# Expert 6's rest rows and ins moved ahead of expert 7's first layer, and with them the clearing, the read-back and the branch of expert 7, in a routed two-expert MoE behind chunked attention

## The chip, the cores and the metric

One core of a Trainium2 chip. The metric is device time in microseconds (us) of one launch of the whole program, the median of several runs. Beside it stands one profiled execution, whose trace is read below. Engines are called as the profile calls them: PE (matmul), PEld (its weight loads), DVE (vector), ACT (scalar), POOL (GpSimd, which here mainly issues DMAs), SP (which issues transposing DMAs). A q behind an engine's name (POOLq) is its sequencer, which handles branches, semaphore waits and the like.

## The reference, cut to what matters

Attention in chunks gives x of 3072 rows by 512. Then each row goes to the two experts (of 8) with the highest noisy logits:

```
top2 = np.argpartition(-noisy_logits, 2, axis=1)[:, :2]
top2_w = softmax of the two logits
for e in range(E):                  # E = 8, D = 512, F = 1024
    for k in range(2):
        mask = top2[:, k] == e
        h = np.maximum(x[mask] @ w1[e], 0.0)
        out[mask] += top2_w[mask, k, None] * (h @ w2[e])
```

## The kernel before

The first part of the program (attention, gating, sorting of the rows) is not touched. It ends with every row on one of 28 lists, one for each pair of experts. Of a list the first 96 rows (MT) are its **main** rows. What a list holds beyond that is a **rest** row, handled once for each of its two experts.

The pairs are numbered so that an expert e has three lists that it shares with the next three experts, its **outs** (`out_of(e)`), three that it shares with the three before it, its **ins** (`in_of(e)`), and one that it shares with expert e+4 or e-4, its **q** list. The work of an expert is

- `mm1_main(e, out_of(e), hO)` and `mm1_main(e, in_of(e), hI)`: first layer for three lists at once (288 columns, 32 matmuls). ACT and DVE in turn apply the relu and write hO or hI. Four PSUM buffers (`p_h`) stand between PE and them.
- `mm1_rest(e, r=False)` and `mm1_rest(e, q=False)`: first layer of the q list, whose 96 rows are spread, 32 each, behind the 96 rows of the three lists in hO; and of the rest rows, 96 of which go behind the lists in hI and 64 to a buffer hB. For the rest rows ACT alone applies the relu (`engs=(0,)`).
- `outs(e)` and `ins_(e)`: second layer, by `mm2_tiles`: for each of three lists a **tile** of 8 matmuls of 128 rows (96 of the list, 32 q or rest rows) by 512. DVE (L1105) adds the 96 rows to what the pair's other expert left, and ACT (L1090) copies the other 32 rows aside, into `yr`. Then PE may use the tile's PSUM buffer again. There are two of these (`p_y`). `ins_(e)` has a fourth, shorter tile, `rest_tile`, for the 64 rows of hB (16 matmuls, L1151), which takes a `p_y` buffer too.
- `scale_q(e)` (DVE, L1128) and `finish_q(e)` (DVE, L1135): weight of the q rows and sum of its two experts, into `yq`.

Results go to DRAM by `put` (L983) and `put_rest` (L1000), one indirect DMA each, issued on POOL; the puts of main rows are collected in a list `later`, which `flush()` issues. A rest row has another expert's share in DRAM already: `clear_prev(e)` (ACT, L1180) fills two tiles pA and pB with zeros, `get_prev(e)` (POOL, L1009) gathers into them what stands in DRAM, and DVE adds the new share: yB (L1157, 64 rows in halves, with pB) and yr (L1171, 96 rows, with pA). These gathers wait until the rest puts of the expert before have landed.

All engines run what they are given in a fixed order (`manual_schedule`): the order in which the code below issues it. Behind the last expert stands a second block: every engine loads a count `nov` into a register (L1523) and branches (L1525). With a count over zero, `overflow()` would run; with this data the branch goes past it. At the join, POOL waits for all its earlier DMAs and raises their semaphores by what `overflow()` would have raised them (`INC_SWDGE_SEM` in the trace). Then `flush()` issues on POOL what is left in `later`.

The loop over experts before, with n = e + 1: `mm1_main(e, in)`, `clear_prev(e)`, gather of the next expert's rest rows, `flush()`, `get_prev(e)`, `outs(e)`, `mm1_rest(e, q=False)`, `mm1_main(n, out)`, `mm1_rest(n, r=False)`, `finish_q(e)`, `flush()`, `ins_(e)`. For the last expert (e = 7): `mm1_rest(7, q=False)`, `mm1_main(7, in)` with `clear_prev(7)` in its middle, `flush()`, `get_prev(7)`, `ins_(7)`, `outs(7)`, `finish_q(7)`; its nine puts are all left for the last `flush()`.

Of the kernel before, what the change touches and what calls it, by code (L numbers as in the profile page):

```python
# [23 lines left out]
def kernel(  # L24
# [21 lines left out]
    N = B * S  # L46
# [53 lines left out]
    MT = 96  # L100
# [946 lines left out]
    def in_of(e):  # L1047
        return [3 * ((e - 1 - k) % E) + k for k in range(3)]
# [13 lines left out]
    def mm1_main(e, ps, h, **kw):  # L1062
        for k0, r in runs(ps):
            n = len(r)
            st = r[1] - r[0] if n > 1 else 1
            stop = r[-1] + (1 if st > 0 else -1)
            sl = slice(r[0], stop if stop >= 0 else None, st)
            mm1(e, n * MT, lambda kp: xs[:, sl, kp, :] if n > 1 else xs[:, r[0], kp, :],
                [(0, n * MT, lambda f0, fk: h[:, f0:f0 + fk, k0:k0 + n, 0:MT])], **kw)
# [16 lines left out]
    later = []  # L1086
# [24 lines left out]
    def flush():  # L1111
        for f in later:
            f()
        later.clear()
# [28 lines left out]
    def ins_(e):  # L1143
        wA, wB, dA, dB, hA, hB_ = rest_of[e]
        pA, pB = prev.pop(e) if e else (None, None)

        def rest_tile():
            p = psY.tile([128, Dm], F32, name="p_y")[:, 0:Dm // 2]
            for f in range(FB):
                for g in range(2):  # L1150
                    nc.tensor.matmul(out=p[g * RU:(g + 1) * RU], lhsT=hB[:, f, :], rhs=w2(e, f, g * Dm // 2, Dm // 2),  # L1151
                                     start=(f == 0), stop=(f == FB - 1), tile_position=(0, g * RU))
            yB = yrp.tile([128, Dm // 2], F32, name="yB", bufs=1)
            if e == 0:
                nc.vector.tensor_scalar(out=yB, in0=p, scalar1=wB, scalar2=None, op0=Alu.mult)
            else:
                nc.vector.scalar_tensor_tensor(out=yB, in0=p, scalar=wB, in1=pB, op0=Alu.mult, op1=Alu.add)  # L1157
            return yB

        unit = yrp.tile([128, Dm], F32, name="yr")  # L1160
        mm2_tiles(e, in_of(e), hI, unit)
        if e == E - 2:
            flush()
        yB = rest_tile()
        later_rest = [partial(put_rest, yB, dB, outB, 2 * N), partial(put_rest, unit[0:MT], dA, out, N)]
        if e < E - 1:
            later_rest.pop(0)()
        if e == 0:
            nc.vector.tensor_scalar(out=unit[0:MT], in0=unit[0:MT], scalar1=wA, scalar2=None, op0=Alu.mult)
        else:  # L1170
            nc.vector.scalar_tensor_tensor(out=unit[0:MT], in0=unit[0:MT], scalar=wA, in1=pA[0:MT], op0=Alu.mult, op1=Alu.add)  # L1171
        if e < E - 1:
            later_rest.pop(0)()
        later.extend(later_rest)

    def clear_prev(e):
        pA = yrp.tile([128, Dm], F32, name="pA", bufs=1)
        pB = yrp.tile([128, Dm // 2], F32, name="pB", bufs=1)
        for to in (pA, pB):
            nc.scalar.copy(to, zero.to_broadcast(list(to.shape)))  # L1180
        prev[e] = (pA, pB)

    def get_prev(e):
        pA, pB = prev[e]
        get_rest(pA[0:MT], rest_of[e][4], out, N)
        get_rest(pB, rest_of[e][5], outB, 2 * N)
# [9 lines left out]
    def turn_q(e):  # L1196
        g = QP + e % 4
        pin(nc.sync.dma_start_transpose(out=x3[e % 2][:, :, 0:MT], in_=xt[g][0:MT]))
# [229 lines left out]
    with tc.manual_schedule(engines={ET.PE, ET.Activation, ET.DVE, ET.SP, ET.Pool}):  # L1428
# [45 lines left out]
        ins_(0)  # L1474
        for e in range(1, E):
            n = e + 1
            if n == E:
                mm1_rest(e, q=False, engs=(0,))
            if n == E:
                mm1_main(e, in_of(e), hI, amid={2: lambda: clear_prev(e)})  # L1480
            else:
                mm1_main(e, in_of(e), hI)
                clear_prev(e)
            if e in (1, 3):
                dx = rest_decode(n, 4 if e == 1 else E)
                for _ in range(3):
                    next(dx)
            new = gathers(in_of(e + 2)) + gathers(out_of(e + 2)) if e + 2 < E else []
            if e + 2 < 4:
                gather_main(QP + e + 2)  # L1490
            if n < E:
                rest_rows(n)
            flush()
            get_prev(e)
            load_next()
            if n == E:
                ins_(e)
            scale_q(e)
            outs(e)
            if n < E:  # L1500
                turn_rest(n)
            turns(new)
            if e + 2 < E:
                turn_q(e + 2)
            if n < E:
                mm1_rest(e, q=False, engs=(0,))
                mm1_main(n, out_of(n), hO)
                mm1_rest(n, r=False)
            finish_q(e)
            if n < E:  # L1510
                flush()
            if e == 1:
                for k in range(4, E):
                    rest_facts(k)
            load_next()
            if n < E:
                ins_(e)
# [40 lines left out]
```

## Time and profile before

| | us |
|---|---|
| median of 3 runs | 334.56 (334.29 to 336.42) |
| the profiled execution | 333.11 |
| its span, first to last instruction | 331.5 |
| outside of the span | 1.6 |
| PE busy | 278.4 (84%) |
| DVE, ACT, POOL busy | 185.7, 153.5, 209.0 |
| mean granted PE clock | 0.926 |

Times in the rows are us from the span's start. The views read below are the chain of work that ended last (followed back from the last instruction), the timeline of one engine (start, length, line, operation, and in brackets how long the engine was idle before it and what the profile takes for the releaser), and the instructions of one source line with those of the sequencers. The first matmul of the experts' first layer (L1032) starts at 127.4 us; the rows below are of the last 52 us, experts 6 and 7.

### The profile page before, as it was taken

To read this page: it belongs to the slowest core of one execution; us is meant where nothing else is said; L and a number is where in the kernel's file an instruction comes from. 1 tells how busy PE (TensorE), PEld (TensorE's weight loads), DVE (VectorE), ACT (ScalarE), POOL (GpSimd) and SP (SyncE) were. 2 spreads that over 40 slices of the span, in tenths; PEclk is the share of its full clock that TensorE was granted. 3 is DMA by queue.
4 is the path that set the end of the run, shared out by engine and by line. 5 is a ranking of instruction groups with operands and counts; after the bars stand their busy time and mean duration, and the time that the engine had idled before them with its cause. 6 is when DMAs were issued, how large, how long until landed. Compare 5 with 4: busy or idle time off the path is not lost.

```text
span 331.5 us, 9214 instructions
## 1 busy us (share of the span) xinstructions
PE 278.4 (84%) x3746; PEld 206.3 (62%) x3762; DVE 185.7 (56%) x418; ACT 153.5 (46%) x316; POOL 209.0 (63%) x304
## 2 busy tenths in 40 slices
PE   0566979888799578999999999999999999999920
PEld 0455867777677368866766775585676666767400
DVE  4765755979798885644653443835345345443520
ACT  5666644766676202535453453453543534525210
POOL 4679595999482457767768675743754744735370
PEclk9969797999979755999999999999999999999975
DMA  7999959988926513435587895998979789522141
GB/s 126 212 211 192 216 109 219 219 138 119 225 51 117 132 30 80 97 79 111 86 182 123 87 182 120 191 217 143 224 151 215 171 158 186 130 83 74 58 145 37
DMA packets 43501, 46.79 MB, mean 141 GB/s; under 512 B 20465, under 2 KB 33845, under 8 KB 43452
## 3 DMA queue, kind: packets, MB, share of 16 engines
q0 software_dynamic: 23024, 38.27, 60.3%
q1 hardware_dynamic: 19884, 7.83, 11.7%
q8 instruction: 31, 0.51, 0.6%
q14 instruction: 18, 0.15, 0.1%
q10 hardware_dynamic: 544, 0.03, 0.1%
HBM read 59.11 MB, written 11.33 MB: 212 GB/s over the span
## 4 chain that ended last, share of the span: by engine, by line
PE 59%; DMA 6%; DVE 6%; issue 3%; ACT 2%; POOL 1%; POOLq 0%; SPq 0%; DVEq 0%; ACTq 0%
PE p_h L1032 28%; PE p_y L1096 21%; DMA w_all<-mvn 5%; PE p_y L1151 2%; PE p_v L490 1%; POOL out_dram L983 1%; PE ps_o L630 1%; ACT pT L616 1%; PE p_t L461 1%; DMA xt<-xd,main_src 1%; ACT w_all L465 1%; PE p_xt L1204 1%; PE p_p L610 0%; PE p_x L652 0%; PE p_rank L338 0%
## 5 line engine op out<-in xcount | busy, mean ns | idle before, releaser
L1032 PE MATMUL p_h<-w_all 128*128 128x288 bf16 (+3 forms) x1120 | 97.5, 248 | 0.7 <-ACT w_all L465 0.5
L1032 PEld LDWEIGHTS <-w_all 128*128 128x128 bf16 x1120 | 83.6, 99 | 14.0 <-issue 2.1
L1096 PE MATMUL p_y<-w_all 128*128 128x512 bf16 x368 | 83.6, 379 | 2.1 <-DVE yq L1090 0.8
L1020 ACT ACTIVATE w_all<-p_h 128x288 bf16<-128x288 f32 (+3 forms) x137 | 46.8, 375 | 45.4 <-PE p_h L1032 42.3
L1096 PEld LDWEIGHTS <-w_all 128*128 128x128 bf16 x384 | 37.1, 98 | 43.6 <-issue 2.1
L437 POOL COPY w_all<-w_all 128x512 bf16<-128x512 bf16 (+1 forms) x59 | 42.9, 795 | 12.2 <-PE p_t L461 7.4
L1018 DVE TENSOR_SCALAR w_all<-p_h 128x288 bf16<-128x288 f32 (+1 forms) x65 | 30.7, 476 | 34.2 <-PE p_h L1032 34.0
L983 POOL DMA_INDIRECT out_dram<-y,main_dst x24 | 22.8, 949 | 18.6 <-DMA w_all<-in_moe_w_dram 5.8
L1105 DVE SCALAR_TENSOR_TENSOR y<-p_y,main_w,y 96x512 f32<-96x512 f32 x24 | 17.9, 747 | 26.0 <-PE p_y L1096 26.0
L978 POOL DMA_INDIRECT xt<-xd,main_src x28 | 26.0, 928 | 10.0 <-issue 7.0
L1090 ACT COPY yr<-p_y 32x512 f32<-32x512 f32 x24 | 13.9, 579 | 36.4 <-DVE y L1105 34.6
L1101 ACT ACTIVATE y<-p_y,main_w 96x512 f32<-96x512 f32 x24 | 16.4, 683 | 21.5 <-PE p_y L1096 21.5
L461 PE MATMUL p_t<-identf,w_all 128*128 128x128 f32 x120 | 19.0, 297 | 1.8 <-ACT pT L616 0.8
L1000 POOL DMA_INDIRECT out_dram<-yB,rd x8 | 9.3, 1160 | 16.8 <-DVE yB L1157 15.6
L1090 DVE COPY yr<-p_y 32x512 f32<-32x512 f32 x12 | 8.3, 694 | 19.8 <-ACT y L1101 19.8
L1262 POOL DMA_INDIRECT fr<-tdr,adr x16 | 16.0, 1000 | 4.9 <-issue 4.6
L978 POOL DMA_INDIRECT xt<-xd,rs x16 | 14.8, 925 | 6.7 <-issue 3.4
L490 PE MATMUL p_v<-identf,w_all 128*128 128x128 f32 x96 | 16.4, 312 | 2.8 <-ACT w_all L465 1.8
L643 DVE TENSOR_TENSOR w_all<-ps_o,rs 128x512 bf16<-128x512 f32 x24 | 15.7, 683 | 5.0 <-PE ps_o L630 4.2
L461 PEld LDWEIGHTS p_t<-identf,w_all 128*128 128x128 f32 x120 | 14.3, 152 | 3.5 <-issue 1.6
L465 ACT COPY w_all<-p_v 128x512 f32<-128x512 f32 x21 | 12.0, 587 | 9.1 <-PE p_v L490 9.0
L1090 DVE COPY yq<-p_y 32x512 f32<-32x512 f32 x12 | 8.3, 694 | 12.9 <-ACT y L1101 12.8
(237 smaller groups left out, 419.6 us busy)
## 6 DMA issues: line engine op xcount, KB each, us to landing
w_all<-in_moe_w_dram POOLq DMA_DIRECT2D x12, 1024.0 KB
w_all<-in_moe_w_dram POOLq DMA_DIRECT2D x16, 256.0 KB
w_all<-in_k_dram POOLq DMA_DIRECT2D x4, 768.0 KB
w_all<-in_q_dram POOLq DMA_DIRECT2D x4, 768.0 KB
w_all<-in_v_dram POOLq DMA_DIRECT2D x4, 768.0 KB
xd<-w_all SPq DMA_DIRECT2D x24, 128.0 KB
w_all<-mvn SPq DMA_DIRECT2D x24, 32.0 KB
w_all<-xt SPq DMA_TRANSPOSE x39
```

Of the source, the lines that this page charges most:

```text
L437: i = eng.tensor_copy(to, x)
L461: nc.tensor.transpose(out=p_t[:, s, :], in_=m.bitcast(F32)[:, s * 128:(s + 1) * 128], identity=identf)
L490: nc.tensor.transpose(out=p_v[:, i, c, :], in_=vT[:, c, c0:c0 + 128], identity=identf)
L978: pin(nc.gpsimd.indirect_dma_start(out=t[0:n].bitcast(I32), out_offset=None, in_=src_, in_offset=bass.IndirectOffsetOnAxis(ap=ix, axis=0)))
L983: i = nc.gpsimd.indirect_dma_start(out=out if rows is None else rows, out_offset=bass.IndirectOffsetOnAxis(ap=ix, axis=0), in_=y, in_offse ...
L1018: nc.vector.tensor_scalar(out=out_, in0=in_, scalar1=0.0, scalar2=None, op0=Alu.max)
L1020: nc.scalar.activation(out=out_, in_=in_, func=Act.Relu)
L1032: nc.tensor.matmul(out=o if len(xk.shape) == 2 else o.rearrange("p (j t) -> p j t", j=xk.shape[1]), lhsT=w_all[:, e % WR, kp * F + f * 128 ...
L1090: (nc.scalar.copy if eng else nc.vector.tensor_copy)(to, p[MT:128, :])
L1096: nc.tensor.matmul(out=p, lhsT=h[:, f, k, :], rhs=w2(e, f), start=(f == 0), stop=(f == FB - 1))
L1101: nc.scalar.activation(out=y[0:MT], in_=p[0:MT], func=Act.Copy, scale=wt)
L1105: nc.vector.scalar_tensor_tensor(out=y[0:MT], in0=p[0:MT], scalar=wt, in1=y[0:MT], op0=Alu.mult, op1=Alu.add)
```

## The change

Only the last two experts are touched. For e = 6 the order becomes: `mm1_main(6, in)`, `clear_prev(6)`, `flush()`, `get_prev(6)`, **`mm1_rest(6, q=False)`**, `outs(6)`, **`finish_q(6)`, `flush()`, `ins_(6)`, `flush()`**, `mm1_main(7, out)` with **`clear_prev(7)` in its middle, `get_prev(7)`**, `mm1_rest(7, r=False)`. For e = 7: `mm1_rest(7, q=False)`, `mm1_main(7, in)`, `ins_(7)` with its **`rest_tile` ahead of the three tiles**, `outs(7)`, `finish_q(7)`. In `ins_(6)` the put of the third list is held back behind the two rest puts.

```diff
@@ ins_ @@
+        if e == E - 1:
+            yB = rest_tile()
+            later.append(partial(put_rest, yB, dB, outB, 2 * N))
         unit = yrp.tile([128, Dm], F32, name="yr")
         mm2_tiles(e, in_of(e), hI, unit)
         if e == E - 2:
+            after = later.pop()
             flush()
-        yB = rest_tile()
-        later_rest = [partial(put_rest, yB, dB, outB, 2 * N), partial(put_rest, unit[0:MT], dA, out, N)]
+            later.append(after)
         if e < E - 1:
-            later_rest.pop(0)()
+            yB = rest_tile()
+            put_rest(yB, dB, outB, 2 * N)
...
+        later.append(partial(put_rest, unit[0:MT], dA, out, N))
         if e < E - 1:
-            later_rest.pop(0)()
-        later.extend(later_rest)
+            later.pop()()
@@ the loop over experts @@
             n = e + 1
+            before_last = n == E - 1
             if n == E:
                 mm1_rest(e, q=False, engs=(0,))
-            if n == E:
-                mm1_main(e, in_of(e), hI, amid={2: lambda: clear_prev(e)})
-            else:
-                mm1_main(e, in_of(e), hI)
+            mm1_main(e, in_of(e), hI)
+            if n < E:
                 clear_prev(e)
...
             if n < E:
                 rest_rows(n)
-            flush()
-            get_prev(e)
+                flush()
+                get_prev(e)
             load_next()
             if n == E:
                 ins_(e)
+            elif before_last:
+                mm1_rest(e, q=False, engs=(0,))
             scale_q(e)
             outs(e)
...
+            if before_last:
+                finish_q(e)
+                flush()
+                load_next()
+                ins_(e)
+                flush()
+                mm1_main(n, out_of(n), hO, amid={1: lambda: clear_prev(n)})
+                get_prev(n)
+                mm1_rest(n, r=False)
+                continue
             if n < E:
                 mm1_rest(e, q=False, engs=(0,))
                 mm1_main(n, out_of(n), hO)
```

**POOL, from expert 6's puts to the branch.** Before; `y` are puts of lists, `yB` and `yr` the rest puts, `pA` and `pB` the gathers of `get_prev(7)`, `nxt` the count that the branch tests:

```order
L983 DMA out_0_dram<-yq_4116,main_dst_3203 3072x512 [waits DMASW6_49,DVE_49]
L983 DMA out_0_dram<-y_5072,main_dst_3203 3072x512 [waits DMASW7_49,DVE_49]
L983 DMA out_0_dram<-y_4777,main_dst_3203 3072x512 [waits DMASW0_49,DVE_49]
L983 DMA out_0_dram<-y_4483,main_dst_3203 3072x512 [waits DMASW1_49,DVE_49]
L1000 DMA out_0_dram<-yB_5604,rd4_4404 6144x256 [waits DMASW2_49,DVE_49]
L1000 DMA out_0_dram<-yr_5544,rd4_4404 3072x512 [waits DMASW3_49,DVE_49]
L1009 DMA pA_5674<-out_0_dram,ri4_4406 96x512 [waits DMASW3_49,DMASW4_49,DMASW2_49,Activation_49]
L1009 DMA pB_5675<-out_0_dram,ri4_4406 128x256 [waits DMASW5_49,Activation_49]
L1523 TENSOR_LOAD nxt_3020 [waits DVE_49]
L1525 COMPARE_AND_BRANCH
```

And in the changed kernel:

```order
L983 DMA out_0_dram<-yq_4116,main_dst_3203 3072x512 [waits DMASW6_49,DVE_49]
L983 DMA out_0_dram<-y_5072,main_dst_3203 3072x512 [waits DMASW7_49,DVE_49]
L983 DMA out_0_dram<-y_4777,main_dst_3203 3072x512 [waits DMASW0_49,DVE_49]
L1000 DMA out_0_dram<-yB_5517,rd4_4404 6144x256 [waits DMASW1_49,DVE_49]
L1000 DMA out_0_dram<-yr_5460,rd4_4404 3072x512 [waits DMASW2_49,DVE_49]
L983 DMA out_0_dram<-y_4483,main_dst_3203 3072x512 [waits DMASW3_49]
L1009 DMA pA_5540<-out_0_dram,ri4_4406 96x512 [waits DMASW2_49,DMASW4_49,DMASW1_49,Activation_49]
L1009 DMA pB_5541<-out_0_dram,ri4_4406 128x256 [waits DMASW5_49,Activation_49]
L1538 TENSOR_LOAD nxt_3020 [waits DVE_49]
L1540 COMPARE_AND_BRANCH
```

The number of rows is the same. One list's put has gone behind the two rest puts; that the whole piece stands earlier against the other engines is seen only on these.

**POOL, from the join to the end of the program.** Before, behind the branch that skips `overflow()`:

```order
L1525 ISA [waits Pool_49,Pool_sequencer_49,DMASW4_49,DMASW5_49,DMASW3_49,DMASW6_49,DMASW2_49,DMASW7_49,DMASW1_49,DMASW0_49]
L1525 UNCONDITIONAL_BRANCH
L983 DMA out_0_dram<-y_5379,main_dst_3203 3072x512 [waits DMASW6_49,DVE_49]
L983 DMA out_0_dram<-y_5084,main_dst_3203 3072x512 [waits DMASW7_49,DVE_49]
L983 DMA out_0_dram<-y_4789,main_dst_3203 3072x512 [waits DMASW0_49,DVE_49]
L1000 DMA out_0_dram<-yB_5766,rd4_4404 6144x256 [waits DMASW1_49,DVE_49]
L1000 DMA out_0_dram<-yr_5715,rd4_4404 3072x512 [waits DMASW2_49,DVE_49]
L983 DMA out_0_dram<-y_3579,main_dst_3203 3072x512 [waits DMASW3_49,DVE_49]
L983 DMA out_0_dram<-y_3975,main_dst_3203 3072x512 [waits DMASW4_49,DVE_49]
L983 DMA out_0_dram<-y_4320,main_dst_3203 3072x512 [waits DMASW5_49,DVE_49]
L983 DMA out_0_dram<-yq_4449,main_dst_3203 3072x512 [waits DMASW6_49,DVE_49]
```

In the changed kernel, the first rows of the same piece (the last four are the same):

```order
L1540 ISA [waits Pool_49,Pool_sequencer_49,DMASW4_49,DMASW5_49,DMASW3_49,DMASW6_49,DMASW2_49,DMASW7_49,DMASW1_49,DMASW0_49]
L1540 UNCONDITIONAL_BRANCH
L1000 DMA out_0_dram<-yB_5732,rd4_4404 6144x256 [waits DMASW6_49,DVE_49]
L983 DMA out_0_dram<-y_5423,main_dst_3203 3072x512 [waits DMASW7_49,DVE_49]
L983 DMA out_0_dram<-y_5084,main_dst_3203 3072x512 [waits DMASW0_49,DVE_49]
L983 DMA out_0_dram<-y_4789,main_dst_3203 3072x512 [waits DMASW1_49,DVE_49]
L1000 DMA out_0_dram<-yr_5734,rd4_4404 3072x512 [waits DMASW2_49,DVE_49]
```

Nine puts stand behind the join in both; yB has gone from fourth to first. The ISA row is `INC_SWDGE_SEM`.

**DVE, expert 7's second layer.** Before: the three ins, the rest rows yB and yr, the scaling of q, the three outs, the sum of q:

```order
L1105 SCALAR_TENSOR_TENSOR y_5379<-p_y_5716,main_w_3208,y_5379 96x512 [waits DMASW0_49,PE_49]
L1105 SCALAR_TENSOR_TENSOR y_5084<-p_y_5727,main_w_3208,y_5084 96x512 [waits PE_49]
L1105 SCALAR_TENSOR_TENSOR y_4789<-p_y_5738,main_w_3208,y_4789 96x512 [waits PE_49]
L1157 SCALAR_TENSOR_TENSOR yB_5766<-p_y_5749,rg4_4405,pB_5675 128x256 [waits DMASW2_49,DMASW5_49,DVE_49,PE_49]
L1171 SCALAR_TENSOR_TENSOR yr_5715<-yr_5715,rg4_4405,pA_5674 96x512 [waits DMASW4_49,Activation_49]
L1128 TENSOR_SCALAR yq_4449<-yq_4449,main_w_3208 96x512
L1105 SCALAR_TENSOR_TENSOR y_3579<-p_y_5771,main_w_3208,y_3579 96x512 [waits PE_49]
```

In the changed kernel:

```order
L1157 SCALAR_TENSOR_TENSOR yB_5732<-p_y_5715,rg4_4405,pB_5541 128x256 [waits DMASW1_49,DMASW5_49,DVE_49,PE_49]
L1105 SCALAR_TENSOR_TENSOR y_5423<-p_y_5735,main_w_3208,y_5423 96x512 [waits DMASW0_49,PE_49]
L1105 SCALAR_TENSOR_TENSOR y_5084<-p_y_5746,main_w_3208,y_5084 96x512 [waits PE_49]
L1105 SCALAR_TENSOR_TENSOR y_4789<-p_y_5757,main_w_3208,y_4789 96x512 [waits PE_49]
L1175 SCALAR_TENSOR_TENSOR yr_5734<-yr_5734,rg4_4405,pA_5540 96x512 [waits DMASW4_49,Activation_49]
L1128 TENSOR_SCALAR yq_4449<-yq_4449,main_w_3208 96x512
L1105 SCALAR_TENSOR_TENSOR y_3579<-p_y_5771,main_w_3208,y_3579 96x512 [waits PE_49]
```

yB, which waits for the landing of pB (DMASW5), has gone from behind the three ins to ahead of them; yr and the scaling of q now follow the third in directly. On SP the order is the same.

## Prediction

> **What bounds the kernel now.** I read the chain that ended last first, from expert 6 on (start, length, what):
>
> ```profile
> 279.85 0.22 PE p_y L1096
> 280.12 4.91 PE p_y L1096 x22
> 285.03 7.49 PE p_h L1032 x96
> 292.58 5.13 PE p_y L1096 x23
> 297.71 0.99 PE p_y L1151 x16
> 298.70 6.24 PE p_h L1032 x64
> 304.94 0.22 PE p_y L1096
> 305.21 4.93 PE p_y L1096 x22
> 310.16 0.76 DVE y L1105
> 310.94 0.59 ACT yr L1090
> 311.56 0.75 DVE yr L1171
> 312.33 0.43 POOL out_dram L983
> ...
> 322.62 0.92 POOL out_dram L983
> ```
>
> Up to 310 us the chain is PE, piece after piece without a hole. Then it leaves PE, and from 312.33 on it is POOL alone. PE works until 316.91 (below), so the end isn't set by the matmuls but by POOL's puts. Their timeline:
>
> ```profile
> 301.30 0.93 POOL L1000 DMA_INDIRECT out_dram<-yr,rd  x1 [0.30 <-issue]
> 304.99 1.00 POOL L1009 DMA_INDIRECT pA<-out_dram,ri  x1 [2.76 <-ACT w_all L1020]
> 306.29 1.03 POOL L1009 DMA_INDIRECT pB<-out_dram,ri  x1 [0.30 <-issue]
> 312.33 1.19 POOL L983 DMA_INDIRECT out_dram<-y,main_dst  x1 [5.01 <-DVE yr L1171]
> ...
> 322.62 0.92 POOL L983 DMA_INDIRECT out_dram<-yq,main_dst  x1 [0.30 <-issue]
> ```
>
> POOL idles 5.01 us and then issues nine puts, the last eight 1.29 us apart on average ((322.62 - 312.33) / 8), the last with only 0.30 behind the one before: it is late with all of them. The profile names DVE's yr as what ended the idle time. But the first put's data is an in of expert 7, whose tile ended at 306.67 (304.94 to 305.21 + 4.93 for three tiles: 1.73 a tile), while yr is the fifth put. So I asked for the branch's line and the end's, sequencers included (count, lengths min/median/max, first and last start):
>
> ```profile
> L1525 POOLq EVENT_SEMAPHORE  x6: 17/30/43, 309.1 to 309.6; - x6
> ...
> L1525 POOLq COMPARE_BRANCH  x1: 58/58/58, 306.0 to 306.0; - x1
> L1525 POOLq INC_SWDGE_SEM  x1: 1735/1735/1735, 309.7 to 309.7; - x1
> ...
> L1525 ACTq COMPARE_BRANCH  x1: 50/50/50, 318.3 to 318.3; - x1
> ...
> L1525 ACTq EVENT_SEMAPHORE  x1: 17/17/17, 320.8 to 320.8; - x1
> L1553 POOLq DRAIN  x3: 46/109/11514, 319.1 to 331.2; - x3
> ```
>
> There it is: POOL branches at 306.0, next does something at 309.1, raises semaphores from 309.7 to 311.4, and starts the first put 0.9 later. That the releaser ended at 312.30 is chance. From branch to first put is **6.3 us**. ACT shows the same hole behind its branch (318.3 to 320.8) with nothing to wait for, so about 3 of the 6.3 us are the branch's own and not the landing of pB.
>
> **The change part by part.** No instruction is added or removed; pieces swap places.
>
> *PE.* The pieces from 279.85 on, by these rows: tiles of outs 5.18, ins 5.13, rest tile 0.99. First layer: the rest rows and ins of 7 take 6.24; the rest rows of 6 with the outs and q rows of 7 take 7.49. Three lists in 32 matmuls take 4.03 (the ins of 6, the row of the same chain just ahead of those above):
>
> ```profile
> 275.83 4.03 PE p_h L1032 x32
> ```
>
> That leaves 2.21 for rest rows and 1.25 for q rows. New order: rest 6 to 282.06, outs 6 to 287.24, ins 6 to 292.37, rest tile 6 to 293.36, first layer of 7 (4.03 + 1.25 + 2.21 + 4.03) to 304.88. Before it is 304.94: **0**, if nothing new stalls. Two places are tight. ACT gets expert 6's eight rest relus right behind the last in's relu and the clears, before the first out's `y`; four PSUM buffers take the four rest tiles, so PE doesn't wait, and ACT is done (about 283.4) when the first out's tile is (283.8). `finish_q(6)` now stands on DVE between outs and ins of 6 and holds the first in's sum by some 0.4 us, so its PSUM buffer comes free at about 290.7, just when the third tile wants it. And expert 7's clears now wait for yr of 6 (294.55), and ACT's next relu for the clears (1.0 us): its `p_h` buffer is free at 295.8, wanted at 295.9. I take 0.05 for these, bounds 0 and 0.5 (one PSUM stall as it stands in the row of 311.57 below, 0.46). Covers gone: beyond these margins each 0.1 us costs 0.1.
>
> *POOL up to the branch.* The puts of 6 stand behind the gathers and puts that fill POOL until 290.5:
>
> ```profile
> 279.44:290.51 11.07, 11.02 (x87) 7.50 (x86) 4.37 (x8) 5.79 (x17) 8.63 (x9) 1.00 0.53 135
> ```
>
> (9 of POOL's DMAs in 11.07 us, so 1.23 each.) The yq put goes at 290.8, two y at 292.0 and 293.3, yB at 294.5 (its data is done at 293.9), yr at 295.8, the third y at 297.0. pA waits for yr's landing: before, 304.99 - 301.30 = 3.69 after yr's start, so 299.5; pB at 300.8. The branch's hole and join then let the first put go 6.3 us after a branch at 300.5: **306.85**, bounds 303.9 (no hole of 3 us) and 309.5 (the hole twice). [...]
>
> *Expert 7's second layer.* Rows before:
>
> ```profile
> 311.16 0.48 DVE L1157 SCALAR_TENSOR_TENSOR yB<-p_y,rg,pB 128x256 f32<-128x256 f32 x1 [0.25 <-PE p_y L1151]
> 311.56 0.74 DVE L1171 SCALAR_TENSOR_TENSOR yr<-yr,rg,pA 96x512 f32<-96x512 f32 x1
> 312.22 0.48 DVE L1128 TENSOR_SCALAR yq<-yq,main_w 96x512 f32<-96x512 f32 x1
> 313.49 0.75 DVE L1105 SCALAR_TENSOR_TENSOR y<-p_y,main_w,y 96x512 f32<-96x512 f32 x1 [0.80 <-PE p_y L1096]
> ...
> 318.34 0.75 DVE L1135 SCALAR_TENSOR_TENSOR yq<-yr,main_w,yq 96x512 f32<-96x512 f32 x1 [0.65 <-ACT yr L1090]
> 311.57 5.34 PE L1096 MATMUL p_y<-w_all 128*128 128x512 bf16 x23 [0.46 <-ACT yr L1090]
> ```
>
> Before, PE stood 0.46 us ahead of the outs: the short rest tile ran out before ACT had emptied the third in's PSUM buffer. Now the rest tile goes first (304.94 to 305.94) and the ins end at 307.67, 309.40 and 311.13, with no stall. But what's late next comes at once. The third in's `y` and copy (0.75 + 0.58) end at 312.5, yr at 313.3, the scaling at 313.7, and only then does DVE take the first out, done by PE at 312.86. Its `y` and ACT copy end at 314.98, and the third out's tile, which wants that buffer, waits for them from 314.6. It starts at 315.03 and ends 1.88 later (like 311.57 to the first out's end, 313.45): **316.91, where it ended before** (311.57 + 5.34). The 0.46 is lost again. So yq is done at 319.09 as before (318.34 + 0.75); if expert 6 loses 0.05, at 319.14.
>
> *The last puts.* A put that finds POOL free starts 0.28 after its data (yq of expert 6: 292.36 + 0.74 to 293.38):
>
> ```profile
> 292.36 0.74 DVE L1135 SCALAR_TENSOR_TENSOR yq<-yr,main_w,yq 96x512 f32<-96x512 f32 x1
> 293.38 0.92 POOL L983 DMA_INDIRECT out_dram<-yq,main_dst  x1 [2.87 <-DVE yq L1135]
> ```
>
> With a first put at 306.85, POOL follows the tiles: yB 306.85, ins at 308.7, 310.5, 312.2, yr 313.6, outs at 314.9, 316.1, 318.0, and the last at 319.42 against 322.62: **3.20 us earlier**. POOL by itself would need the first put by 309.5 for that (319.42 less eight steps of 1.23), so it has 2.7 us in hand. The first put of before took 1.19 instead of 0.92 beside L1128; yr's put will run beside it, so I allow it 0.3, which the gaps behind it take up. [...]
>
> *Behind the last put.* From its end (323.54) to the span's end are 7.96 us, most of it POOL's DRAIN (319.1 to 330.6). I carry these, and the 1.6 outside of the span, along unchanged. The profiled execution would go from 333.11 to 329.9. The median of the runs shown is 1.45 above it; the difference is applied to it: 334.56 - 3.20 = **331.4**.
>
> **The rivals.**
>
> 1. *POOL stays behind.* The hole behind the branch, or the wait for the landings of yB and yr ahead of pA, takes over 2.7 us more than here, and the puts queue again. For it: POOL's piece up to the branch is full from 279.4 on. Against: POOL has to be late for eight puts. Up to half of the gain goes: 332 to 333.5.
> 2. *The end doesn't follow the last put.* DRAIN starts at 319.1, just when yq is done and long before the last put's start, and takes 11.51. If that length is its own, not a wait for the puts, the end stays with yq: 334.6. Against: four puts were still due at 319.1, and a drain that waits for them explains a start ahead of them.
> 3. *Slower: pB lands late.* DVE's yB waits for pB and now stands ahead of all six tiles. DVE takes its work in order, so a late pB holds the `y` of the ins, their PSUM buffers and PE. By the sum pB is issued at 300.8 and landed by 304.1 (before: started 306.29, its semaphore passed by 309.6), and is wanted at 306.0. PE first feels it when the second in's tile wants the rest tile's buffer, at 307.7. Slower than before begins where pB lands 3.2 us after that slack, at some 310.4, over 6 us late. If the gather waited for the landing of every put before it in a crowded queue, say until 314, the time would be 338.
> 4. *More than forecast.* If the third out's stall stays away, or part of the 7.96 shrinks once the puts no longer queue, 0.5 to 1.5 more: 330 to 330.9.
>
> That the change doesn't do what it says is unlikely: in the order, the branch stands right behind pB, and pB right behind expert 6's puts.
>
> **How the numbers follow.** Forecast 0.62, alone 330.9 to 331.9 (the tight PE places on one side, half a stall less on the other); rivals 0.12, 0.12, 0.06 and 0.08. The range from 329.9 to 334.5 takes in the first and the fourth rival and part of the second, leaving out about 0.16. One per cent, about what a measurement of this kernel can tell from no change, is 3.35 us, so 331.2: the forecast lies just inside. Of it 0.28 is below 331.2; with the fourth rival 0.36 faster. The rest of it and the first two rivals make 0.58 the same; the third, 0.06 slower.
>
> **What would show it.** In the profile after: the idle time of 5.01 ahead of the first put behind the join gone, POOLq's branch at 300 to 301, its join's INC_SWDGE_SEM ended by 306; yB's put first, at about 306.9; the last put at 319 to 320, waiting for yq and not for POOL; PE's first layer of 7 ended at 304.9 to 305.1; PE idle about 0.45 ahead of the third out and not of the first; 8 us from the last put's end to the span's. Wrong I am if INC_SWDGE_SEM ends after 309, if the 8 us change by over 0.5, or if DVE's yB waits for a DMA.

## The result, and the profile after

The changed kernel takes **332.14 us** (median of 20 runs, 329.45 to 335.07), the kernel before 334.55 in the same session (20 runs, 331.65 to 339.91). The ratio is 0.9932, 95% interval 0.9904 to 0.9960: some 2.3 us less, 1.3 to 3.2 by the interval. Forecast were 331.4 and 3.2 less. Ratios, here and below, leave out slowed runs, over 1.5% above the fastest of their kernel, so they can differ a little from the ratio of two medians.

| profiled execution, us | before | forecast | after |
|---|---|---|---|
| time / span | 333.11 / 331.5 | 329.9 / - | 330.17 / 328.5 |
| POOL's branch | 306.0 | 300.5 | 300.5 |
| first put behind it | 312.33 | 306.85 | 307.08 |
| PE's first layer of 7 ends | 304.94 | 304.93 | 305.03 |
| last put starts | 322.62 | 319.42 | 319.59 |
| its end to the span's end | 7.96 | 7.96 | 7.96 |

POOL's timeline of the changed kernel, from the last puts of expert 6 on (start, length, what, in brackets the idle time ahead of it):

```profile
295.88 0.93 POOL L1000 DMA_INDIRECT out_dram<-yr,rd  x1 [0.30 <-DVE w_all L1018]
297.11 0.92 POOL L983 DMA_INDIRECT out_dram<-y,main_dst  x1 [0.30 <-issue]
299.55 1.00 POOL L1009 DMA_INDIRECT pA<-out_dram,ri  x1 [1.51 <-ACT w_all L1020]
300.85 1.03 POOL L1009 DMA_INDIRECT pB<-out_dram,ri  x1 [0.30 <-ACT w_all L1020]
307.08 1.02 POOL L1000 DMA_INDIRECT out_dram<-yB,rd  x1 [5.20 <-DVE yB L1157]
308.92 0.95 POOL L983 DMA_INDIRECT out_dram<-y,main_dst  x1 [0.81 <-DVE y L1105]
310.64 0.92 POOL L983 DMA_INDIRECT out_dram<-y,main_dst  x1 [0.77 <-DVE y L1105]
312.37 0.92 POOL L983 DMA_INDIRECT out_dram<-y,main_dst  x1 [0.81 <-DVE y L1105]
313.76 0.92 POOL L1000 DMA_INDIRECT out_dram<-yr,rd  x1 [0.47 <-DVE yr L1175]
314.98 0.92 POOL L983 DMA_INDIRECT out_dram<-y,main_dst  x1 [0.30 <-issue]
316.21 0.92 POOL L983 DMA_INDIRECT out_dram<-y,main_dst  x1 [0.30 <-issue]
318.20 0.92 POOL L983 DMA_INDIRECT out_dram<-y,main_dst  x1 [1.07 <-DVE y L1105]
319.59 0.92 POOL L983 DMA_INDIRECT out_dram<-yq,main_dst  x1 [0.48 <-DVE yq L1135]
```

The idle time of about 5 us is still there, but it now lies ahead of the work. Before, 0.30 stood between all the puts (a queue). Now 0.5 to 1.1 do, with a DVE row named: POOL waits for tiles. Only the two puts behind yr's still stand 0.30 apart, and the queue is empty again before the third out's. The branch and the end, in the view of one line with its sequencers:

```profile
L1540 POOLq COMPARE_BRANCH  x1: 58/58/58, 300.5 to 300.5; - x1
L1540 POOLq INC_SWDGE_SEM  x1: 1735/1735/1735, 304.4 to 304.4; - x1
...
L1568 POOLq DRAIN  x3: 46/109/8257, 319.4 to 328.2; - x3
```

The end of the chain that ended last:

```profile
285.39 0.76 DVE y L1105
...
293.07 12.97 DMA out_dram<-y,main_dst
306.28 0.58 issue
307.08 1.02 POOL out_dram L1000
...
318.20 0.92 POOL out_dram L983
319.11 0.24 issue
319.36 1.15 POOLq L1568
```

It now leaves PE at 285.39 and runs through the join. The 12.97 us are no landing: that put's data had landed by 295.81, and 293.07 + 12.97 is 306.04, when the join's INC_SWDGE_SEM raises the same semaphore. So this chain is not what bounds: the first put could have gone earlier without moving the last one, as the kernel without the branch shows below.

The hole is as long as it was, 6.5 us from branch to first put (307.08 - 300.54) against 6.3. PE and DVE in expert 7's second layer:

```profile
304.96 1.06 PE L1151 MATMUL p_y<-w_all 128*64 128x256 bf16 x16
305.95 8.81 PE L1096 MATMUL p_y<-w_all 128*128 128x512 bf16 x40
315.25 1.89 PE L1096 MATMUL p_y<-w_all 128*128 128x512 bf16 x8 [0.49 <-ACT yr L1090]
...
306.06 0.48 DVE L1157 SCALAR_TENSOR_TENSOR yB<-p_y,rg,pB 128x256 f32<-128x256 f32 x1 [1.03 <-DMA out_dram<-yB,rd]
...
312.74 0.75 DVE L1175 SCALAR_TENSOR_TENSOR yr<-yr,rg,pA 96x512 f32<-96x512 f32 x1 [0.65 <-ACT yr L1090]
313.40 0.48 DVE L1128 TENSOR_SCALAR yq<-yq,main_w 96x512 f32<-96x512 f32 x1
...
318.56 0.75 DVE L1135 SCALAR_TENSOR_TENSOR yq<-yr,main_w,yq 96x512 f32<-96x512 f32 x1 [0.65 <-ACT yr L1090]
```

PE's stall has moved from ahead of the first out to ahead of the third, 0.49 long, and yq is done at 319.31. The mean granted clock is 0.943 against 0.926 before, but rows of the same work are equally long in the experts' part of both: 1.06 for a rest tile, 6.31 for 64 matmuls of the first layer. So the clock is not what shortened the last stage.

### The profile page after: what moved, and what is told of

It is laid out like the page before. It is cut to its first block, busy times and chain, and to the rows that moved or that the text cites. A ratio compares the mean times of both kernels' runs of the same rounds, so it can differ in the third digit from the quotient of the medians.

```text
span 328.5 us, 9225 instructions
## 1 busy us (share of the span) xinstructions
PE 279.1 (85%) x3762; PEld 205.7 (63%) x3762; DVE 185.5 (56%) x418; ACT 153.4 (47%) x316; POOL 210.3 (64%) x304
## 4 chain that ended last, share of the span: by engine, by line
PE 49%; DMA 9%; DVE 8%; POOL 6%; issue 4%; ACT 2%; POOLq 1%; DVEq 0%; ACTq 0%
PE p_h L1032 24%; PE p_y L1096 18%; DMA out_dram<-y,main_dst 4%; POOL out_dram L983 3%; DMA w_all<-mvn 2%; DMA xd<-w_all 2%; PE p_y L1151 2%; PE p_t L461 1%; POOL w_all L378 1%; POOL red L364 1%; DMA xt<-xd,main_src 1%; PE p_list L384 1%; DVE w_all L532 1%; ACT pb L603 1%; ACT pT L616 1%
## 5 line engine op out<-in xcount | busy, mean ns | idle before, releaser
L1032 PE MATMUL p_h<-w_all 128*128 128x288 bf16 (+3 forms) x1120 | 96.4, 247 | 0.9 <-DVE w_all L1018 0.5
L1032 PEld LDWEIGHTS <-w_all 128*128 128x128 bf16 x1120 | 82.8, 99 | 14.0 <-issue 2.5
L1096 PE MATMUL p_y<-w_all 128*128 128x512 bf16 x384 | 85.9, 379 | 1.2 <-DVE yq L1090 0.6
L1105 DVE SCALAR_TENSOR_TENSOR y<-p_y,main_w,y 96x512 f32<-96x512 f32 x24 | 17.9, 746 | 23.5 <-PE p_y L1096 23.5
L1101 ACT ACTIVATE y<-p_y,main_w 96x512 f32<-96x512 f32 x24 | 16.4, 683 | 22.0 <-PE p_y L1096 19.9
L461 PE MATMUL p_t<-identf,w_all 128*128 128x128 f32 x120 | 18.2, 287 | 1.6 <-ACT pT L616 0.8
```

Source lines behind the costliest of these rows:

```text
L461: nc.tensor.transpose(out=p_t[:, s, :], in_=m.bitcast(F32)[:, s * 128:(s + 1) * 128], identity=identf)
L1032: nc.tensor.matmul(out=o if len(xk.shape) == 2 else o.rearrange("p (j t) -> p j t", j=xk.shape[1]), lhsT=w_all[:, e % WR, kp * F + f * 128 ...
L1096: nc.tensor.matmul(out=p, lhsT=h[:, f, k, :], rhs=w2(e, f), start=(f == 0), stop=(f == FB - 1))
L1101: nc.scalar.activation(out=y[0:MT], in_=p[0:MT], func=Act.Copy, scale=wt)
L1105: nc.vector.scalar_tensor_tensor(out=y[0:MT], in0=p[0:MT], scalar=wt, in1=y[0:MT], op0=Alu.mult, op1=Alu.add)
```

## The experiments

My theory: the gain is POOL's time behind the branch, taken out of the way of expert 7's puts by the earlier clearing, read-back and branch; the rest tile's new place brings nothing by itself. The rival: it is the new order of tiles (PE's stall), and the branch is beside the point.

Single executions differ by several us in parts that no edit touches (in the profiled ones expert 0's first matmul starts anywhere from 127.4 to 134.1 us), so I compare the last stage. **L** is the start of the last put, **S** the end of the span, both counted from the end of the last L1032 matmul, which is where expert 7's first layer ends. The first four variants below (from "before, no branch" to "sums of yr and q moved") ran on a chip on which the kernel before takes 334.8 us; the others on two chips on which it takes 417 and 422. There PE waits for "issue" in the first layer's line, as in this row from the list of waits of the first kernel with early scaling (total us, times, longest),

```profile
PE p_h L1032 <- issue: 22.2, 19, 3.7
```

while all the idle time ahead of that group is 0.9 us in the changed kernel's profile above. That hides a gain of two us in the total, but not in the last stage.

| kernel | L | S | ratio to before, 95% |
|---|---|---|---|
| before | 17.68 | 26.56 | |
| after | 14.56 | 23.44 | 0.9932 [0.9904, 0.9960] |
| before, no branch | 14.42 | 23.22 | 0.9821 [0.9762, 0.9880] |
| after, no branch | 14.56 | 23.37 | 0.9931 [0.9880, 0.9981] |
| after, late clearing and branch | 15.93 | 24.81 | 0.9944 [0.9891, 0.9996] |
| after, sums of yr and q moved | 14.73 | 23.61 | 0.9891 [0.9831, 0.9951] |
| after, rest tile behind the ins | 14.43 | 23.30 | 0.9998 [0.9937, 1.0059] |
| before, rest tile first (two runs) | 16.41, 16.38 | 25.29, 25.25 | 1.0128 [0.9916, 1.0339], 0.9942 [0.9840, 1.0043] |
| after, rest rows of 6 behind the outs | 14.56 | 23.44 | 0.9987 [0.9940, 1.0033] |
| after, last puts by SP | - | 19.27 | 0.9962 [0.9879, 1.0045] |
| after, scaling of q early (three runs) | 14.17 | 23.05 | 1.0032 [0.9958, 1.0105], 0.9891 [0.9819, 0.9964], 0.9931 [0.9888, 0.9975] |

### Without the branch

```diff
-        with tc.issue_after(last[0].ins):
-            nov = nc.values_load(nxt[0:1, 0:1], ...
-        with tc.If(nov > 0):
-            overflow()
```

In the kernel before:

> The kernel before without the count's load, the branch and the overflow path behind it (left out: the rows beyond the rest rows' room, of which this data has none). Theory (the gain of the change is POOL freed from the branch's hole before expert 7's puts are due): the first put behind pB starts at about 307.7 instead of 312.33, the puts then follow the tiles, the last starts at 319.4 instead of 322.6, span 328.3, ratio to before 0.990: the whole gain without any reordering. Rival (the gain is in the new order of PE's work): no change, 331.5.

and in the changed one:

> The changed kernel without the branch (same part left out). Theory: in the changed kernel the hole behind the branch is hidden (POOL is ready at about 307.0, when yB is), so the last put stays at 319.6 and the span at 328.5, within 0.2. Rival (the branch still costs something there, at the end of the program too): 0.5 or more shorter.

POOL's timeline of the kernel before without its branch:

```profile
309.73 1.03 POOL L1009 DMA_INDIRECT pB<-out_dram,ri  x1 [0.30 <-issue]
311.18 0.95 POOL L983 DMA_INDIRECT out_dram<-y,main_dst  x1 [0.42 <-DVE y L1105]
...
315.85 1.18 POOL L1000 DMA_INDIRECT out_dram<-yB,rd  x1 [0.31 <-DVE yr L1171]
...
322.81 0.91 POOL L983 DMA_INDIRECT out_dram<-yq,main_dst  x1 [0.48 <-DVE yq L1135]
```

The order is the old one, late gathers included, yet the first put goes 0.42 behind pB and the last waits for yq. L is 14.42: taking the branch away gives the whole gain of the change in the last stage (3.26 against 3.12) without moving a tile. In the changed kernel the same edit gives nothing (14.56 both). So the two are one gain, and the rival falls. What the edit takes out is the whole block: the count's load, the branch, and the join with its waits and INC_SWDGE_SEM. The runs don't part these. The new order itself costs a little: from the start of expert 5's rest tile to the last put are 44.60 us in the old order without the branch, 45.00 in the new one with it or without. The total of the first, 329.75 us (6 runs), is 5.1 below the kernel before, 1.8 more than its last stage explains (by the ratio of the table it would be 6.0 below); its profiled execution (333.48) doesn't contain it, and it stays open.

### Late clearing and branch in the changed order

```diff
-            mm1_main(e, in_of(e), hI)
+            mm1_main(e, in_of(e), hI, **(dict(amid={2: lambda: clear_prev(e)}) if n == E else {}))
+            if n == E:
+                get_prev(e)
...
-                mm1_main(n, out_of(n), hO, amid={1: lambda: clear_prev(n)})
-                get_prev(n)
+                mm1_main(n, out_of(n), hO)
```

> The changed kernel with expert 7's clearing (and with it the read-back) back in the middle of the first layer of its ins, the rest tile still ahead of the ins. Theory: pA starts at 303.3 (the clearing's end) instead of 299.55, pB at 304.6, the branch at 304.3, the first put at about 310.6; pB lands at about 307.7, so DVE's yB ends at 308.3 instead of 306.5 and PE stalls some 0.7 ahead of the second in; the nine puts need the first by 309.5, so the last starts at 320.4: 0.8 to 1.0 later than in the changed kernel, 2.0 to 2.3 earlier than before. Rival (where the clearing stands does not matter): as the changed kernel, 328.5.

```profile
308.16 1.03 POOL L1009 DMA_INDIRECT pB<-out_dram,ri  x1 [0.30 <-ACT w_all L1020]
314.22 1.02 POOL L1000 DMA_INDIRECT out_dram<-yB,rd  x1 [5.02 <-DVE y L1105]
315.55 0.96 POOL L983 DMA_INDIRECT out_dram<-y,main_dst  x1 [0.31 <-issue]
316.81 1.25 POOL L983 DMA_INDIRECT out_dram<-y,main_dst  x1 [0.30 <-issue]
...
324.50 0.92 POOL L983 DMA_INDIRECT out_dram<-yq,main_dst  x1 [0.30 <-issue]
```

The branch comes at 307.84, 0.7 us ahead of the layer's end, instead of 4.5 ahead of it, and the queue of 0.30 gaps is back. 1.37 of the 3.12 are lost again, more than I had expected, since one put is also stretched. The third rival shows itself in small: DVE's yB waits for pB, and PE's next row of 40 matmuls takes 9.04 instead of 8.81, so it lost 0.23 where 0.7 had been expected.

```profile
310.93 0.48 DVE L1157 SCALAR_TENSOR_TENSOR yB<-p_y,rg,pB 128x256 f32<-128x256 f32 x1 [2.36 <-DMA pB<-out_dram,ri]
```

### The place of the rest tile

In the changed kernel put back behind the ins:

```diff
-        if e == E - 1:
-            yB = rest_tile()
-            later.append(partial(put_rest, yB, dB, outB, 2 * N))
         unit = yrp.tile([128, Dm], F32, name="yr")
...
+        else:
+            yB = rest_tile()
+            later.append(partial(put_rest, yB, dB, outB, 2 * N))
```

> The changed kernel with expert 7's rest tile put back behind its ins. Counted from the end of the first layer of expert 7's ins (305.0 in the changed kernel): theory (that the rest tile goes first gains nothing by itself): PE stalls 0.46 ahead of the first out as before, and not ahead of the third; the last put starts 14.4 after, as in the kernel before without its branch, against 14.56 in the changed one; the span ends at 23.3 against 23.44. Rival (putting the rest tile first is part of the gain): last put 15.0 or later.

In the kernel before put ahead of them (the opposite edit), run twice:

> The kernel before with nothing changed but expert 7's rest tile ahead of its ins. Theory: the branch stands where it did, so the first put starts 7.4 after the end of expert 7's first layer, the nine puts queue and the last starts at 17.7, as before (17.68): no gain. DVE's yB now waits for pB's landing until about 4.4, so PE stalls some 2.2 ahead of the second in, which the puts' queue hides; yq is done at 16.3 to 16.5. Rival (the gain is in the new order of the second layer): last put at 15 or earlier; rival (the late pB costs): later than 18.2.

> The kernel before with the rest tile of expert 7 first, once more. On the slow chip the branch stood 0.23 ahead of the end of the first layer, since PE itself was held there, and the last put came 16.64 after the branch, the same as before (322.62 - 305.98 = 16.64). Theory: where PE isn't held the branch is 1.0 after the first layer's end as before, the last put 17.7 after it, the span ends 26.6 after it: no gain, ratio 0.995 to 1.005. Rival (the rest tile's place gains by itself): 16.4 or less.

With the rest tile last the stall ahead of the first out is back, as expected (0.45), and L is 14.43, 0.13 less than in the changed kernel. With it first in the kernel before, L reads 16.4 both times, the figure that had been put down for the rival. But the condition of that figure, a PE that isn't held, was met in neither run: PE stood for 0.16 and 0.78 (0.18 and 0.79 in the first run) waiting for ACT within the first layer just ahead, and so the branch came 0.2 ahead of the layer's end instead of 1.0 behind it. From branch to last put the two runs take 16.64 and 16.60 (before: 322.62 - 305.98 = 16.64), and POOL's puts stand 0.30 apart to the end. PE pays for yB waiting for pB, as the second of these runs shows:

```profile
391.32 1.90 PE L1096 MATMUL p_y<-w_all 128*128 128x512 bf16 x8
393.75 7.07 PE L1096 MATMUL p_y<-w_all 128*128 128x512 bf16 x32 [0.53 <-DVE yB L1157]
```

So the tile's place gains nothing. In the changed order it costs a tenth: on one chip L is 14.56 with it first (the variant below) and 14.43 with it last.

### Rest rows of expert 6 behind its outs

```diff
-            elif before_last:
-                mm1_rest(e, q=False, engs=(0,))
             scale_q(e)
             outs(e)
...
             if before_last:
+                mm1_rest(e, q=False, engs=(0,))
                 finish_q(e)
```

> The changed kernel with expert 6's rest rows' first layer put back behind its outs (but still ahead of its ins). Theory (their place ahead of the outs is neither needed nor harmful: PE does the same work, and the ins find the relus done): from the end of the first layer of expert 6's ins to that of expert 7's ins 25.1 to 25.3 as in the changed kernel, last put 14.56 after that. Rival (the ins of 6 wait for ACT's relus of the rest rows when these come right ahead of them): 0.3 to 0.6 longer.

The last stage is that of the changed kernel (14.56 and 23.44), as it should be. From the end of the first layer of expert 6's ins to that of expert 7's are 35.1, neither the 25.1 to 25.3 of the theory nor the rival's 0.3 to 0.6 more. In expert 6's ins PE waited twice for ACT:

```profile
371.20 1.03 PE L1096 MATMUL p_y<-w_all 128*128 128x512 bf16 x2 [2.68 <-ACT w_all L1020]
375.42 7.71 PE L1096 MATMUL p_y<-w_all 128*128 128x512 bf16 x22 [3.19 <-ACT w_all L1020]
```

But ACT itself stood idle there for 2.94 and 3.73 us with nothing of this core named, on one of the slower chips. Whether the order or the chip made these waits isn't settled, nor what the rest rows' place ahead of the outs is worth.

### What bounds the last stage now

First, the sum of yr behind the first out's, and the scaling of q ahead of the rest tile:

```diff
-                ins_(e)
...
+                scale_q(e)
+                outs(e, amid={0: ins_(e)})
```

(`ins_` hands back yr's sum as a function, called behind the first out.)

> The changed kernel with two of DVE's sums of expert 7 moved out of the way of its first out: the scaling of q ahead of the rest tile's sum, the rest rows' sum yr behind the first out's y. Theory: DVE takes the first out as soon as PE ends it (313.1 instead of 313.8), so the stall of 0.49 ahead of the third out goes, PE ends at 316.6 instead of 317.1, yq is done at 318.8 and the last put starts at 319.1: 0.5 earlier than in the changed kernel, span 328.0, ratio to before 0.989. Rival (the last put is held by POOL, which then has yr's put behind the first out's): no change to the changed kernel.

PE's 48 matmuls run through in one row of 10.53 and yq is done 0.64 sooner, but the last put 0.17 later: yr's put now stands behind an out's, and two puts are stretched.

```profile
317.53 1.18 POOL L983 DMA_INDIRECT out_dram<-y,main_dst  x1 [0.81 <-DVE y L1105]
...
321.46 1.43 POOL L983 DMA_INDIRECT out_dram<-y,main_dst  x1 [0.30 <-issue]
323.19 0.92 POOL L983 DMA_INDIRECT out_dram<-yq,main_dst  x1 [0.30 <-issue]
```

POOL is the bound again by a hair, as the rival had it. So only the scaling is moved, yr stays:

```diff
             if n == E:
+                scale_q(e)
                 ins_(e)
-            elif before_last:
-                mm1_rest(e, q=False, engs=(0,))
-            scale_q(e)
-            outs(e)
+                outs(e)
+            else:
+                if before_last:
+                    mm1_rest(e, q=False, engs=(0,))
+                scale_q(e)
+                outs(e)
```

> The changed kernel with one of DVE's operations moved: the scaling of q of expert 7 ahead of the rest tile's sum. Theory: DVE takes the first out 0.4 sooner, PE's stall of 0.49 ahead of the third out shrinks to 0.1 or less, yr's put stays ahead of the outs' and starts beside no operation of DVE that reads only SBUF, so no put is stretched (in the run with both sums moved two were, by 0.26 and 0.51, and POOL took back the 0.6 that PE gained). Last put 14.0 after the end of expert 7's first layer instead of 14.56, span end 22.85 instead of 23.44. Rival (POOL's five last puts are the bound whatever DVE does): 14.5.

> The kernel with the scaling of q moved ahead of the rest tile's sum, once more: the run before found its chip a quarter slower in the whole expert part (before: 417 us), so that its total says little. Its last part measured 14.17 from the end of expert 7's first layer to the last put and 23.05 to the span's end. Theory: the same here within 0.1, so some 0.4 shorter than the changed kernel there (14.56, 23.44), and a ratio to before of 0.988 to 0.993. Rival (the 0.4 was the slow chip's doing): 14.5 and 23.4.

> The changed kernel with the scaling of expert 7's q issued ahead of its ins, a third time. If what its two earlier executions showed belongs to the kernel and not to the chip, then from the end of expert 7's first layer the last put starts after 14.1 to 14.3 us and the span ends after 22.9 to 23.2, against 14.56 and 23.44 of the changed kernel. Against the kernel before, time is 2.3 to 3.8 us shorter: the changed kernel's gain of 2.3 to 3.0, and 0.4 more. If the early scaling only moves the wait, the last put starts after 14.5 or more.

L is 14.17 and S 23.05 in each of the three, 0.39 less than in the changed kernel. That is less than the 0.56 expected: of PE's stall a quarter of a us is left (the 48 matmuls take 10.79, against 10.53 where both sums were moved). The last put waits for yq:

```profile
393.14 10.79 PE L1096 MATMUL p_y<-w_all 128*128 128x512 bf16 x48
...
404.99 0.91 POOL L983 DMA_INDIRECT out_dram<-y,main_dst  x1 [0.67 <-issue]
406.38 0.92 POOL L983 DMA_INDIRECT out_dram<-yq,main_dst  x1 [0.48 <-DVE yq L1135]
```

This has the shortest last stage of the kernels that do all the work. The totals don't tell it from the changed kernel: ratios to before from 0.9891 to 1.0032 on the slower chips, the third (0.9931 [0.9888, 0.9975]) right at the changed kernel's own. I take the 0.4 us as shown in the stage and not in the time.

### The last puts by another engine

The nine last puts are left out; SP stores the tiles into a scratch buffer instead, so POOL has nothing left to issue behind its join.

```diff
-        flush()
+        sink = tc.dram_tile([9 * 128, Dm], F32, name="sink")
+        for i, f in enumerate(later):
+            y = f.args[0]
+            n, c = y.shape
+            pin(nc.sync.dma_start(out=sink[i * 128:i * 128 + n, 0:c], in_=y))
+        later.clear()
```

> The changed kernel with the nine puts behind the join replaced by nine plain DMAs from SP into a scratch tensor (the rows of these puts do not reach the output). POOL then ends with its join, about 1.1 after the end of expert 7's first layer. Theory (the 8.9 from the last put's start to the span's end are POOL's put and a drain that waits some 7 after POOL's last indirect DMA): the drain is over long before PE is, and the end is set by the last DMA's landing, about 2 after yq is done at 14.3: the span ends 17 to 18 after that point instead of 23.44, some 6 shorter. Rival (the time behind the last put is the end of any program, whoever issues the last DMA): about 23.

S falls by 4.17, to 19.27, so the time behind the last put isn't the end of any program. I had expected 17 to 18: another hole takes its turn, that of DVE's own branch.

```profile
L1573 POOLq DRAIN  x3: 46/103/6362, 390.2 to 408.0; - x3
...
L1540 DVEq COMPARE_BRANCH  x1: 72/72/72, 403.6 to 403.6; - x1
...
L1540 DVEq EVENT_SEMAPHORE  x1: 21/21/21, 407.2 to 407.2; - x1
```

With no put to wait for, DRAIN still takes 6.36, directly behind the join.

## Why the prediction was right, point by point

**The hole and the queue behind it: right, and shown by taking it away.** The branch came at 300.54 (forecast 300.5), the join's INC_SWDGE_SEM ended at 306.15 (by 306), yB's put went first, at 307.08 (306.85). As before the first put goes 0.93 behind the join's end. The 0.23 of lateness cost nothing: the puts behind it wait for tiles. The first rival is dead. One reading within it was too strong: that some 3 of POOL's 6.3 us are the branch's own and not the landing of pB. The last of pB's data lands at 308.94 before and 303.53 after, 0.19 and 0.34 ahead of the join's first row, and the join waits for that landing too. Either would have held POOL for most of the 3 us. The forecast carried the whole hole over unchanged, so the number didn't depend on this. That the hole might stretch, as the upper bound and the first rival had it, was an estimate of mine that no run shows: from the branch to the first put are 6.35 us before (312.33 - 305.98) and 6.54 after.

**PE: the moved stall was right, the tight places were mis-sized.** The stall ahead of the third out is 0.49 (about 0.45 forecast). But from the start of expert 5's rest tile (274.76 before, 274.59 after) to the end of expert 7's first layer are 30.18 us before and 30.43 after. The forecast had 0.01 less than before, with 0.05 for the two tight places included; the order cost 0.25 instead. The figure 30.43 (within 0.01) returns in the three variants of the new order that ran on the first chip, and 30.18 in the kernel before without its branch, so it is the order's. It is lost in expert 6's second layer: its 48 matmuls take 10.78, and 48 that don't stall take 10.53 (expert 7's with both sums moved). DVE shows the wait that was named:

```profile
288.51 0.75 DVE L1135 SCALAR_TENSOR_TENSOR yq<-yr,main_w,yq 96x512 f32<-96x512 f32 x1 [0.65 <-ACT yr L1090]
289.18 0.74 DVE L1105 SCALAR_TENSOR_TENSOR y<-p_y,main_w,y 96x512 f32<-96x512 f32 x1
290.57 0.75 DVE L1105 SCALAR_TENSOR_TENSOR y<-p_y,main_w,y 96x512 f32<-96x512 f32 x1 [0.65 <-PE p_y L1096]
292.55 0.75 DVE L1105 SCALAR_TENSOR_TENSOR y<-p_y,main_w,y 96x512 f32<-96x512 f32 x1 [1.23 <-PE p_y L1096]
```

The first in's sum starts with no idle time behind `finish_q`'s, and the third in's starts 1.98 behind the second's, where 1.73 is a tile's time: the 0.25. The other tight place cost nothing that shows (the 128 matmuls of the first layer behind run in one row). No run moves `finish_q(6)` alone, so this is read from the rows. I took 0.05 of 0 to 0.5, and it was 0.25: that term is the step that was mis-sized. It hides in the last put's 319.59, which lies so near the forecast 319.42 partly by luck: from expert 5's rest tile to the last put are 45.00 instead of 47.86, a gain of 2.86 (3.12 in the last stage less 0.25), and 0.17 more come from parts that no edit touches. The timed 2.3 [1.3, 3.2] agrees with 2.9.

**The end follows the last put: right, and the second rival is dead.** DRAIN went from 11.51 to 8.26, yet it ends 7.1 behind the last put's end in both (330.64 - 323.54 and 327.61 - 320.51). In the kernel before without its branch it starts at 322.6, takes 8.25 and ends 7.1 behind it too. Its start says nothing. In every variant that ends with a put the span's end is 7.9 to 8.0 behind that put's end (S less L less the put's 0.92).

**pB late: right that it wasn't.** DVE's yB names a DMA with 1.03 of idle time, and I had called that a sign of being wrong. But the DMA named is an old put of yB's buffer, long landed, and the sum starts 0.04 behind its tile's modelled end (304.96 + 1.06), as it does in the changed kernel without a branch. By the row alone it looks like the third rival; the releaser's time shows it isn't. With the late clearing above, where pB is late, the row names pB, with 2.36.

**yr's put beside L1128: it wasn't stretched** (0.92), and the 0.3 that I allowed wasn't needed. Why, stands below.

## What to carry over

The branch around code that this data never runs had a price here, with its join, on more engines than one: in the changed kernel's profile 3.3 us from the branch's row to the sequencer's next on POOL (300.55 to 303.87), 2.5 on ACT (318.49 to 321.00), 3.0 on DVE (319.20 to 322.24). Put such a branch where the engine has nothing due, and look for the price in the gap between the branch's row and the next useful one (6.5 us on POOL), not in the branch's own 0.06 us. With the branch in the kernel before, POOL's queue of puts began 4.60 us later behind the first layer's end than without it (7.39 against 2.79) and ended 3.26 later (17.68 against 14.42); the rest was slack of the tiles behind. So the test for the bound is one row: does the last put wait for its data or for the put before it? And count from a fixed point in the trace (here the last first-layer matmul): a gain of 0.4 us read the same three times there, while the totals moved by several.

## What the runs showed of the hardware

- The stretch of POOL's indirect DMAs is not only L1128's. In the kernel before, yB's put in expert 5 starts 0.36 us into a two-input sum from SBUF to SBUF and takes 1.27 instead of 1.02:

```profile
276.27 0.74 DVE L1171 SCALAR_TENSOR_TENSOR yr<-yr,rg,pA 96x512 f32<-96x512 f32 x1
276.63 1.27 POOL L1000 DMA_INDIRECT out_dram<-yB,rd  x1 [4.24 <-DVE yB L1157]
```

  In the rows above, a put of an out takes 1.18 beside yr's sum and 1.43 beside yq's sum (321.35 to 322.10). The stretched puts end 0.8 to 0.9 us behind the end of the DVE operation. In the profiles of the kernel before and of the changed one together, from 200 us on, 10 puts start within such a sum, and all take 1.04 to 1.31. Another 20 start within a DVE operation that reads PSUM (L1105 among them), and none takes over 0.97. A put that starts 0.36 ahead of yq's sum (318.20, 0.92) isn't touched. yr's put in the changed kernel starts only 0.12 ahead of L1128's end: with the 0.8 that makes no more than the 0.92 which it takes anyway.
- POOL's drain ended 7.1 us behind the last put's end in the kernel before, with its branch and without, and in the changed kernel, and took 6.36 where nothing was issued since the join (the last puts by SP). Of the 7.9 to 8.0 us from the last put's end to the span's end it makes the most in these three.
- From the branch to the join's first row are 3.3 us on POOL in the changed kernel (300.55 to 303.87) and 3.6 on DVE in the run with the last puts by SP (403.6 to 407.2). On POOL two things happen in that time that the rows don't name, before as after. An 8 KB transfer on a DMA queue that the profile calls "instruction" starts 1.5 us behind the branch before (307.47) and 1.7 after (302.28), and the join's first row follows 1.7 and 1.6 behind its start. And pB's landing, for which the join waits as well, ends 0.19 and 0.34 ahead of that row. So a branch that cost nothing would have brought POOL's first put forward by some half a us only. That is an estimate, which no run shows: the join's row that waits for pB stands at 304.15 and pB had landed at 303.53; before, at 309.41 and 308.94.
